# RWKV-style attention and a gated MLP on one core: three f-tiles begun with the tokens of steps 0 and 1, the second group's attention placed later, and y made as rows of x from step 3 on

## The chip, the core and the metric

One NeuronCore of a Trainium2 chip runs the whole program. Its engines work side by side, each on its own instruction queue, in order: TensorE (PE in the profile, its weight loads PEld), VectorE (DVE), ScalarE (ACT), GpSimd (POOL) and SyncE (SP), whose queue issues most of the DMAs. The metric is the device time of one execution in microseconds; smaller is better.

## The reference

Two parts follow each other. A linear attention runs over 768 tokens with one 48x48 state for each of 4 batches and 8 heads; its output, 3072 tokens by 384, goes through an MLP of 2048 hidden columns with a gate.

```python
for t in range(S):                       # S = 768, B = 4, H = 8, D = 48
    kt, vt, rt = (k[:, :, t], v[:, :, t], r[:, :, t])
    cur = np.einsum('bhd,bhe->bhde', u[None] * kt, vt)
    y[:, :, t] = np.einsum('bhd,bhde->bhe', rt, state + cur)
    state = w[None, :, :, None] * state + np.einsum('bhd,bhe->bhde', kt, vt)
...
x = np.ascontiguousarray(y.transpose(0, 2, 1, 3)).reshape(B * S, H * D)
h = x @ w_in                             # 384 -> 2048
sp = np.where(h > 20.0, h, np.log1p(np.exp(np.minimum(h, 20.0))))
g = h * np.tanh(sp)
return (g @ w_out).astype(np.float32)    # 2048 -> 384
```

## The kernel before

**The attention** is cut into 24 steps of 128 tokens (64 tokens of two batches). Step s multiplies r and k by tables of powers of w (`scale`, L483, on DVE), makes scores k·r for all heads on PE (`scores`, called from `attend`), keeps the part below the diagonal (L594, copies by a mask on DVE), and moves the pieces into two alternating sets of operands G, Wt and KI (`halves`: by ACT or DVE for steps 0 to 2, by DMAs of SP, L471, afterwards). `outputs(s)` then makes y (from G and Wt) and the new state st (from Wt and KI) on PE; the state goes back into Wt (L680). A step so needs the state of the step before it.

The term with u, which stands on the diagonal, is made in one of two ways. For s < UDIAG (6) the keys times u are scored a second time (`diag`, L504 or L502, and a second call of `scores`), and a second masked copy puts that diagonal in. From UDIAG on DVE works out the diagonal alone (L512, L516, L520, L525) from k and r loaded in the other layout.

**From y to x.** The MLP wants x with its 384 features on partitions. For s < TURN (6) `tokens` makes y with tokens on partitions; ACT copies it out (L693, L695), PE transposes it in three pieces (`transposes`, L751), ACT copies the result into x (L720), and in every group but the first DVE writes a second part (L723). From TURN on `rows` makes y with features on partitions at once; `direct` copies it into x with two ACT copies (L734) and two DVE subtractions (L737), and six small DMAs on SP's queue (L743) put the features of the fourth head pair where they belong.

**The MLP** has eight groups of three steps, 384 tokens each, and 16 f-tiles of 128 hidden columns in each. `up` makes one f-tile of h (hp in PSUM, two buffers), it is copied out (L892), four f-tiles form a batch of gate work on ACT (three activations with their table loads, L813, L816, L819) and DVE (L828), and `down` adds the f-tile to the output (acc, three PSUM tiles). In group 0 up and down are fp32 products with the weights whole (L802, L847: three k-tiles, six records of the profile for each f-tile); from group 1 on, weights and inputs are split in two parts and three products replace one (L778). The weights come as 16 pieces of 64-bit numbers and are converted to fp32 on ACT and DVE (L340 to L368) while group 0 runs, and are split afterwards (L383, L385).

**Who sets the order.** `Flow` is a planner that runs while the program is built. Each thread (load_step, scale, diag, keys, attend, outputs, evacuate, gate, ...) yields the events that it waits for and then what engine it wants and for how long; the planner gives the engine to the thread that can begin first by its cost table, and among equals to the lowest rank. The order that comes out is the order of every engine's queue, and the chip keeps to it whatever the real durations are. `place(s, piece)` says after which up tile (event `u<n>`) a step's scores (piece 0), outputs (piece 1) and, for the last step of a group, transposes (piece 2) may be put on PE: the 16 up tiles of the group before it are used from a share LO to a share HI, for group 1 LO0 and HI0. `rank(s)` follows from `place`, so a later place also means that the step's DVE and ACT work comes behind more of the other work. `ffn` is one thread that gives up tile n and then the down tiles that AFTER allows; in group 0 the first down tile comes after up tile 7. `up_tile` waits for x of the three steps of its group, and the first tile of the third batch (up tile 8) waits until the first batch is gated. While no up tile has been placed, `keep_warm` fills PE's idle time with products of zeros (L283).

At the start `state_decay` writes the diagonal of w**64 into KI[0] (L263, eight ACT instructions), and the thread `second_decay` writes the same into KI[1] by eight more, which `outputs(1)` waits for.

```python
    lo, hi = (LO0, HI0) if g == 1 else (LO1, HI1)
    at = (2 * (s - starts[g]) + piece) / (2 * GROUPS[g])
    return n0 + min(n - 1, int((lo + at * (hi - lo)) * n))
```

Of the kernel before, what the change touches and what calls it, by code (L numbers as in the profile page):

```python
# [22 lines left out]
NP = H // 2  # L23
# [4 lines left out]

TURN = 6


SOON = 3
LENT = 2

UDIAG = 6

# [11 lines left out]
WG = 2  # L48
# [20 lines left out]
LAG_US = 24.9  # L69
LO0, HI0, LO1, HI1 = 0.05, 0.9, 0.05, 0.8  # L70
AHEAD, HOLD_W = 2, 8
# [111 lines left out]
def pe(us):  # L183
    return {"pe": us}
# [3 lines left out]
def rwkv_mish_kernel(ctx, tc, rkT, rkN, vN, wT, w_in, w_out, consts, rkF, vF, wF, uF, outT):  # L188
# [70 lines left out]

    def state_decay(i, par, p):  # L260

        r = DROWS[par]
        nc.scalar.activation(  # L263
            KI[i][r, par, :, p, :], ident[r, r].unsqueeze(1).broadcast_to([D, 2, D]), AF.Copy, scale=w64[r, p : p + 1]
        )
# [11 lines left out]

    idle = ps.tile([128, 512], F32, name="idle", tag="hp", bufs=2)

# [8 lines left out]
    for par in range(2):  # L288
        for p in range(NP):
            state_decay(0, par, p)  # L290
    token_table()
# [4 lines left out]
    ok = const.tile([32, 1], I32, name="ok")  # L296

    def second_decay():
        for par in range(2):
            for p in range(NP):  # L300
                yield {"act": 0.3}
                state_decay(1, par, p)
        flow.set("decay")

# [93 lines left out]
    def load_step(s):  # L398
        i, q = divmod(s, NQ)
        before = s - RK_BUFS - (LENT < s <= LENT + RK_BUFS)  # L400
        if before >= 0 and s != LENT:
            yield f"moved{before}"
            yield f"placed{before}"
            yield f"keys{before}" if before < TURN else f"x{before}"
        yield {"sp": 1.28}
        if not spare:
            spares()
        rk = [128, 2, 2, NP, C]
        n = [128, 2, 2, NP, D]
# [81 lines left out]
    def diag(s):  # L491
        yield f"rkn{s}"
        if s < UDIAG:
            flow.set(f"rku{s}")
            yield f"scaled{s}"
            if s >= 2:
                yield f"scores{s - 2}"
            engine = yield {"act": 0.8, **dve(512)}
            k, to = rks[s][:112, 1], spare["ku"][s % 2][:112]
            if engine == "act":  # L500
                for p in range(NP):
                    nc.scalar.activation(to[:, :, p], k[:, :, p], AF.Copy, scale=uw[:112, p : p + 1])  # L502
# [56 lines left out]
    def attend(s):  # L559
# [6 lines left out]
        if GROUPS[0] <= s < UDIAG:  # L566
            yield f"state{s - 1}"
        if s > TURN:

# [5 lines left out]
        rk = loaded[s][0]  # L575
        if s <= TURN:
            yield from paced(s, 0)
# [52 lines left out]
    def outputs(s):  # L630
        q = s % 2
        last = s >= NS - NQ

        more = TURN <= s < NS - 1
        yield f"moved{s}"
        yield f"placed{s}"
        yield f"keys{s}"
        yield f"v{s}"
        if s == 1:
            yield "decay"  # L640
        if s:
# [84 lines left out]
    def direct(s, y):  # L726
        g, x, at = yield from new_x(s)

        last = loaded[s][1].rearrange("a m c p d -> a (m c p d)")[:, : 2 * ST].rearrange("a (m t) -> a m t", m=2)
        last = last.bitcast(F32R)  # L730
# [25 lines left out]
    def place(s, piece):  # L756

        if s > TURN and not piece:
            return place(s - 1, 1)
# [32 lines left out]
    def by_tile(o, t):  # L792
        return t[:, : o.n * o.T].rearrange("p (j t) -> p j t", j=o.n)

    def up(o, j):
        f, T = o.f + j, o.T
        hp = ps.tile([128, 512], F32, name="hp", tag="hp", bufs=2)
        w = (wholes if o.whole else parts)[0, f // WG]
# [55 lines left out]
    def put(engine, mt, T, cols):  # L854
# [4 lines left out]
        (nc.scalar.copy if engine == "act" else nc.vector.tensor_copy)(out=ob[:, :T], in_=accs[mt][:, :T])  # L859
        nc.scalar.dma_start(outT[mt * 128 : (mt + 1) * 128, cols], ob[:, :T])  # L860

# [3 lines left out]
    def up_tile(n):  # L865
# [9 lines left out]
        if n >= 2:  # L875
            yield f"h{n - 2}"
        yield pe(unit_us(n))
        flow.fill = None
# [96 lines left out]
    flow.start(load_weights(), -500, 0.0)  # L975
    flow.start(second_decay(), -1000.5, 0.0)
    for c in range(len(W_ORDER)):
# [4 lines left out]
        n += NF  # L982
        flow.start(split(c), (AFTER[n] - L_OUT if i else n - L_IN) + c / 1000, 0.0)
    flow.start(ffn(), 1000, 0.0)
    flow.run()
# [153 lines left out]
```

## Time and profile before

| | |
|---|---|
| runs, us | 529.8, 531.26, 535.85 (median 531.26) |
| the profiled execution, us | 530.0 |
| its span in the profile, us | 528.2 |
| mean granted TensorE clock | 0.994 |
| first up tile begins (L802), us from the span's start | 33.94 |
| first down tile begins (L847) | 56.53 |
| first up tile of group 1 (L778) | 101.26 |
| last product ends | 521.91 |

The span is what the profiler saw between the first and the last instruction; the time of that execution is 1.8 us longer. Times in views of the trace are counted from the span's start.

### The profile page before, as it was taken

The page shows a single profiled execution, that of the slowest core. Times are in us where ns is not written, and L with a number is a line of the kernel's source. Part 1 is how long each engine was busy: PE and PEld are TensorE (multiplying, and loading weights), DVE is VectorE, ACT ScalarE, POOL GpSimd, SP SyncE. Part 2 cuts the span into 40 slices and gives each one's busy share as a digit, 9 for nine tenths or more (in the row PEclk, how much of TensorE's full clock was granted, in tenths as well). Part 3 has the DMA queues.
Part 4 walks back from the last instruction along what each step waited for, and adds up shares of the span by engine and source line. Part 5 has one row for each costly group of instructions (what it writes and reads, how often), then busy time and mean ns, then how long its engine had stood idle before and what let it go on. Part 6 is the DMA issues. An engine that isn't in the chain of part 4 may idle for free.

```text
span 528.2 us, 11442 instructions
## 1 busy us (share of the span) xinstructions
PE 510.8 (97%) x4765; PEld 470.1 (89%) x4765; DVE 323.3 (61%) x489; ACT 402.8 (76%) x501; POOL 6.0 (1%) x19
## 2 busy tenths in 40 slices
PE   8887999999999999999999999999999999999994
PEld 6754666687999999999999999999999999999993
DVE  6998998765676575474664475474474473334341
ACT  6999957669798668667887768667687767777882
POOL 4000000000000000000000000000000000000000
PEclk9999899999999999999999999999999999999998
DMA  8998444113443244323443243323333250001001
GB/s 238 414 374 274 130 132 130 45 37 92 115 115 106 59 149 114 86 74 103 119 114 104 63 151 108 97 59 107 117 116 104 66 153 17 2 2 45 1 0 49
DMA packets 31051, 57.88 MB, mean 110 GB/s; under 512 B 6064, under 2 KB 19248, under 8 KB 30992
## 3 DMA queue, kind: packets, MB, share of 16 engines
q1 hardware_dynamic: 27392, 52.13, 33.9%
q10 hardware_dynamic: 3600, 4.95, 2.7%
q8 instruction: 39, 0.64, 0.5%
q14 instruction: 20, 0.16, 0.1%
HBM read 36.80 MB, written 4.72 MB: 79 GB/s over the span
## 4 chain that ended last, share of the span: by engine, by line
PE 80%; ACT 7%; DVE 4%; DMA 3%; SPq 2%; issue 2%; ACTq 0%; DVEq 0%
PE hp L778 30%; PE acc L778 27%; PE hp L802 6%; PE acc L847 5%; PE pa L554 5%; PE yt L620 3%; PE st L664 2%; SPq L743 1%; DMA rk<-in_rkT_dram 1%; ACT fa L816 1%; PE yt L607 1%; ACT wraw L340 1%; DMA rkn<-in_rkN_dram 1%; ACT L819 1%; DVE hb L828 1%
## 5 line engine op out<-in xcount | busy, mean ns | idle before, releaser
L778 PE MATMUL hp<-x,w 128*128 128x384 f32 x1008 | 197.0, 338 | 0.5 <-DMA x<-rkn 0.5
L778 PE MATMUL acc<-gh,w 128*128 128x384 f32 x672 | 187.8, 335 | 1.0 <-ACT gh L831 1.0
L778 PEld LDWEIGHTS hp<-x,w 128*128 128x128 f32 x1008 | 175.6, 188 | 3.8 <-DMA x<-rkn 0.8
L778 PEld LDWEIGHTS acc<-gh,w 128*128 128x128 f32 x672 | 122.8, 188 | 1.4 <-ACT gh L831 1.3
L778 PE MATMUL acc<-gl,w 128*128 128x384 f32 x336 | 112.3, 334 | 0.1
L892 ACT COPY hb<-hp 128x384 f32<-128x384 f32 x100 | 47.3, 474 | 59.6 <-PE hp L778 47.0
L828 DVE TENSOR_TENSOR hb<-hb,fa 128x768 f32<-128x768 f32 (+1 forms) x58 | 51.8, 927 | 39.9 <-ACT fa L819 39.9
L892 DVE COPY hb<-hp 128x384 f32<-128x384 f32 x28 | 15.6, 557 | 86.8 <-PE hp L778 84.1
L778 PEld LDWEIGHTS acc<-gl,w 128*128 128x128 f32 x336 | 63.1, 188 | 0.4 <-DVE gl L834 0.4
L831 ACT CAST gh<-hb 128x768 fp32r<-128x768 f32 (+1 forms) x58 | 47.2, 817 | 21.0 <-DVE hb L828 20.8
L834 DVE TENSOR_TENSOR gl<-hb,gh 128x768 fp32r<-128x768 f32 (+1 forms) x58 | 52.7, 928 | 7.6 <-ACT gh L831 5.8
L813 ACT ACTIVATE fa<-hb,bias_ln 128x1536 f32<-128x1536 f32 (+1 forms) x33 | 50.9, 1541 | 0.4
L816 ACT ACTIVATE fa<-fa 128x1536 f32<-128x1536 f32 (+1 forms) x33 | 47.8, 1449 | 2.0 <-ACT ob L859 1.7
L819 ACT ACTIVATE fa<-fa 128x1536 f32<-128x1536 f32 (+1 forms) x33 | 47.8, 1449 | 0.4
L819 ACT ACT_TABLE_LOAD x33 | 42.3, 1283 | 0.6
L813 ACT ACT_TABLE_LOAD x33 | 42.3, 1283 | 0.6
L483 DVE TENSOR_TENSOR rk<-rk,TRK 112x1024 f32<-112x1024 f32 x23 | 28.1, 1222 | 14.3 <-DMA rk<-in_rkT_dram 14.3
L847 PE MATMUL acc<-g,wraw 128*128 128x384 f32 x96 | 34.5, 496 | 0.0
L802 PE MATMUL hp<-x,wraw 128*128 128x384 f32 x96 | 33.2, 492 | 0.9 <-ACT x L720 0.9
L554 PE MATMUL pa<-rk 48*64 48x64 f32 x736 | 26.6, 222 | 4.7 <-DVE rk L483 3.5
L554 PEld LDWEIGHTS pa<-rk 48*64 48x64 f32 x736 | 23.4, 135 | 7.6 <-DVE rk L483 4.1
L802 PEld LDWEIGHTS hp<-x,wraw 128*128 128x128 f32 x96 | 18.4, 196 | 11.9 <-ACT x L720 1.1
(88 smaller groups left out, 452.5 us busy)
## 6 DMA issues: line engine op xcount, KB each, us to landing
rk<-in_rkT_dram SPq DMA_DIRECT2D x23, 448.0 KB, 4.2
rkn<-in_rkN_dram SPq DMA_DIRECT2D x18, 384.0 KB, 3.9
wraw<-in_w_in_dram SPq DMA_DIRECT2D x8, 768.0 KB, 12.1
wraw<-in_w_out_dram SPq DMA_DIRECT2D x8, 768.0 KB, 15.8
G<-rk SPq DMA_DIRECT2D x36, 128.0 KB, 2.3
out_dram<-ob ACTq DMA_DIRECT2D x24, 192.0 KB, 2.2
Wt<-in_vN_dram SPq DMA_DIRECT2D x46, 96.0 KB, 2.6
G<-rk SPq DMA_DIRECT2D x42, 96.0 KB, 2.4
```

Source lines behind the costliest of these rows:

```text
L483: nc.vector.tensor_tensor(out=rk[:112], in0=rk[:112], in1=TRK[:112].unsqueeze(2).broadcast_to([112, 2, 2, NP, C]), op=ALU.mult)
L554: nc.tensor.matmul(pa[TROWS[par], n : n + C], lhsT=keys[r, c, p, :], rhs=rk[r, 0, c, p, :], start=True, stop=True)
L778: nc.tensor.matmul(out, lhsT=a, rhs=m, start=first and n == 0, stop=last and n == 2)
L802: nc.tensor.matmul(hp[:, :T], lhsT=w[:, fs], rhs=o.x[:, 0, k, :T], start=k == 0, stop=k == KT - 1)
L813: nc.scalar.activation(o.g, o.hb, AF.Sigmoid, bias=bias_ln2, scale=1.0)
L816: nc.scalar.activation(o.g, o.g, AF.Arctan)
L819: nc.scalar.activation(o.g, o.g, AF.Sin, scale=2.0)
L828: nc.vector.tensor_tensor(out=to[:, j], in0=o.hb[:, j], in1=o.g[:, j], op=ALU.mult)
L831: nc.scalar.copy(out=o.gh[:, j], in_=o.hb[:, j])
L834: nc.vector.tensor_tensor(out=o.gl[:, j], in0=o.hb[:, j], in1=o.gh[:, j].bitcast(F32), op=ALU.subtract)
L847: nc.tensor.matmul(accs[mt][:, :T], lhsT=w[:, ws], rhs=o.gh[:, j], start=first, stop=last)
L892: (nc.scalar.copy if engine == "act" else nc.vector.tensor_copy)(out=o.hb[:, j], in_=h)
```

## The change

The order of the work and a few of its parts change; what is computed stays.

- `up_early`: f-tiles 0, 1 and 2 of group 0 are multiplied with the 256 tokens of steps 0 and 1 as soon as x of these is there; `up` then adds only the last 128 tokens. Each such tile is 2 x 3 products in place of 3. Tile 2 is put into the PSUM tile of acc0, and the products of zeros write to acc1 in place of hp.
- TURN goes from 6 to 3: steps 3, 4 and 5 use `rows` and `direct`. JOIN (6) keeps the other role of TURN, which step's scores are issued by the step before.
- UDIAG goes from 6 to 5: step 5 works its diagonal out on DVE.
- LO0 goes from 0.05 to 0.25. By `place`, scores and outputs of steps 3, 4, 5 may come after up tiles 4, 5 / 7, 9 / 10, 12, where before it was 0, 3 / 5, 7 / 9, 12.
- KI[1] is copied from KI[0] by four GpSimd copies (the loop stands twice) in place of the eight ACT instructions of `second_decay`.
- Of the last group's output, what DVE copied out is stored from SP's queue in place of ACT's.

```diff
-TURN = 6
+TURN = 3
+
+JOIN = 6
...
+EARLY = 3
...
-UDIAG = 6
+UDIAG = 5
...
-LO0, HI0, LO1, HI1 = 0.05, 0.9, 0.05, 0.8
+LO0, HI0, LO1, HI1 = 0.25, 0.9, 0.05, 0.8
...
-    idle = ps.tile([128, 512], F32, name="idle", tag="hp", bufs=2)
+    idle = ps.tile([128, 512], F32, name="idle", tag="acc1")
...
+    for par in range(2):
+        r = DROWS[par]
+        nc.gpsimd.tensor_copy(KI[1][r, par], KI[0][r, par])
+    for par in range(2):
+        r = DROWS[par]
+        nc.gpsimd.tensor_copy(KI[1][r, par], KI[0][r, par])
     token_table()
...
-    def second_decay():
-        for par in range(2):
-            for p in range(NP):
-                yield {"act": 0.3}
-                state_decay(1, par, p)
-        flow.set("decay")
...
-            yield f"keys{before}" if before < TURN else f"x{before}"
+            yield f"keys{before}" if before < UDIAG else f"x{before}"
...
+            if s - 2 >= TURN:
+                yield f"x{s - 2}"
...
-        if s > TURN:
+        if s > JOIN:
...
-        if s <= TURN:
+        if s <= JOIN:
...
-        more = TURN <= s < NS - 1
+        more = JOIN <= s < NS - 1
...
-        if s == 1:
-            yield "decay"
...
-        last = loaded[s][1].rearrange("a m c p d -> a (m c p d)")[:, : 2 * ST].rearrange("a (m t) -> a m t", m=2)
+        if s < UDIAG:
+            last = spare["ku"][s % 2].rearrange("a c p i -> a (c p i)")
+        else:
+            last = loaded[s][1].rearrange("a m c p d -> a (m c p d)")
+        last = last[:, : 2 * ST].rearrange("a (m t) -> a m t", m=2)
...
-        if s > TURN and not piece:
+        if s > JOIN and not piece:
...
+    def up_early(n):
+        g, f = UNITS[n][1:]
+        T = 128 * (GROUPS[g] - 1)
+        for s in range(GROUPS[g] - 1):
+            yield f"x{s}"
+        yield f"v0,{f // WG}"
+        yield pe(KT * 4 * T / 2400)
+        hps[n] = hp = ps.tile([128, 512], F32, name="hp", **(dict(tag="hp", bufs=2) if n < 2 else dict(tag="acc0")))
+        whole_up(hp, xs[g], f, slice(0, T))
+        flow.set(f"early{n}")
+
+    def whole_up(hp, x, f, at):
+        w = wholes[0, f // WG]
+        for k in range(KT):
+            fs = slice((k * WG + f % WG) * 128, (k * WG + f % WG + 1) * 128)
+            nc.tensor.matmul(hp[:, at], lhsT=w[:, fs], rhs=x[:, 0, k, at], start=k == 0, stop=k == KT - 1)
+
     def up(o, j):
         f, T = o.f + j, o.T
+        if o.whole and f in hps:
+            hp = hps.pop(f)
+            whole_up(hp, o.x, f, slice(T - 128, T))
+            return hp[:, :T]
...
-        nc.scalar.dma_start(outT[mt * 128 : (mt + 1) * 128, cols], ob[:, :T])
+
+        q = nc.sync if cols.stop == NT and engine == "dve" else nc.scalar
+        q.dma_start(outT[mt * 128 : (mt + 1) * 128, cols], ob[:, :T])
...
-        yield pe(unit_us(n))
+        if n < EARLY:
+            yield f"early{n}"
+        yield pe(unit_us(n) / (GROUPS[g] if n < EARLY else 1))
...
-    flow.start(second_decay(), -1000.5, 0.0)
...
+    for n in range(EARLY):
+        flow.start(up_early(n), n, 0.0)
```

More of the change, by code (lines that the diff above doesn't have):

```diff
@@ L258, in powers, with state_decay @@
             nc.vector.tensor_tensor(out=both(n, C - 2 * n, n), in0=both(0, C - n, n), in1=mul, op=ALU.mult)
-    def state_decay(i, par, p):
+    def state_decay(par, p):
         r = DROWS[par]
         nc.scalar.activation(
-            KI[i][r, par, :, p, :], ident[r, r].unsqueeze(1).broadcast_to([D, 2, D]), AF.Copy, scale=w64[r, p : p + 1]
+            KI[0][r, par, :, p, :], ident[r, r].unsqueeze(1).broadcast_to([D, 2, D]), AF.Copy, scale=w64[r, p : p + 1]
         )
@@ L289, in rwkv_mish_kernel @@
         for p in range(NP):
-            state_decay(0, par, p)
+            state_decay(par, p)
+    for par in range(2):
[4 more added lines that the diff above has]
+        nc.gpsimd.tensor_copy(KI[1][r, par], KI[0][r, par])
     token_table()
@@ L793, in by_tile @@
         return t[:, : o.n * o.T].rearrange("p (j t) -> p j t", j=o.n)
+    hps = {}
+    def up_early(n):
[13 more added lines that the diff above has]
+            nc.tensor.matmul(hp[:, at], lhsT=w[:, fs], rhs=x[:, 0, k, at], start=k == 0, stop=k == KT - 1)
     def up(o, j):
         f, T = o.f + j, o.T
+        if o.whole and f in hps:
+            hp = hps.pop(f)
+            whole_up(hp, o.x, f, slice(T - 128, T))
+            return hp[:, :T]
         hp = ps.tile([128, 512], F32, name="hp", tag="hp", bufs=2)
```

## The prediction

> **What bounds the kernel now.** I read the page first, its busy shares, then the windows of the first 110 us, then the timeline of the same stretch engine by engine, then the waits of PE, and last the timeline's end.
>
> ```profile
> PE 510.8 (97%) x4765; PEld 470.1 (89%) x4765; DVE 323.3 (61%) x489; ACT 402.8 (76%) x501; POOL 6.0 (1%) x19
> ...
> 16.00:24.00 8.00, 7.19 (x199) 6.31 (x197) 7.78 (x15) 7.63 (x14) 0.00 (x0) 1.00 1.02 415
> 24.00:32.00 8.00, 6.49 (x143) 5.41 (x140) 7.38 (x13) 7.85 (x17) 0.00 (x0) 1.00 1.02 346
> ...
> 50.00:52.00 2.00, 0.05 (x1) 0.00 (x0) 1.91 (x3) 1.99 (x2) 0.00 (x0) 1.00 0.41 101
> 52.00:54.00 2.00, 0.43 (x14) 0.43 (x16) 2.00 (x4) 2.00 (x4) 0.00 (x0) 1.00 0.02 7
> 54.00:56.00 2.00, 2.00 (x52) 2.00 (x48) 2.00 (x3) 1.98 (x6) 0.00 (x0) 0.60 0.35 95
> 56.00:58.00 2.00, 2.00 (x15) 1.35 (x12) 2.00 (x4) 1.99 (x2) 0.00 (x0) 0.55 0.44 107
> ```
>
> The page says PE, at 97%; but that is an average. In the windows the columns are start and end, length, then busy time of PE, PEld, DVE, ACT and POOL, the granted clock and the DMA share. Before 34 us the work runs through DVE and ACT, each 92 to 98% busy in 16 to 32 us, while PE's busy time is partly products of zeros. At 50 us PE stands still, and then gets only 0.60 and 0.55 of its clock for two windows of 2 us: 0.40 x 2 + 0.45 x 2 = 1.7 us lost beside the stop. After that PE is full to the end, so there time is PE work. The chain of events at the stop, from the timeline:
>
> ```profile
> 28.21 0.48 ACT L720 COPY x<-t 128x384 f32<-128x384 f32 x1
> 28.46 1.17 PE L607 MATMUL yt<-Wt,G 128*64 128x48 f32 x32
> 30.42 0.72 PE L283 MATMUL idle<-zeros 128*128 128x256 bf16 x5
> 31.99 0.55 PE L751 MATMUL t<-cst,G 128*128 128x128 f32 x3 [0.85 <-ACT G L695]
> 33.41 0.48 ACT L720 COPY x<-t 128x384 f32<-128x384 f32 x1
> 33.94 2.21 PE L802 MATMUL hp<-x,wraw 128*128 128x384 f32 x6 [0.86 <-ACT x L720]
> 36.23 13.82 PE L802 MATMUL hp<-x,wraw 128*128 128x384 f32 x42
> 42.35 0.48 ACT L892 COPY hb<-hp 128x384 f32<-128x384 f32 x1 [0.61 <-PE hp L802]
> 50.89 1.48 ACT L819 ACTIVATE fa<-fa 128x1536 f32<-128x1536 f32 x1
> 52.30 1.22 DVE L483 TENSOR_TENSOR rk<-rk,TRK 112x1024 f32<-112x1024 f32 x1
> 53.57 1.32 PE L554 MATMUL pa<-rk 48*64 48x64 f32 x32 [3.52 <-DVE rk L483]
> 53.91 1.82 DVE L828 TENSOR_TENSOR g<-hb,fa 128x768 f32<-128x768 f32 x2
> 56.53 2.82 PE L847 MATMUL acc<-g,wraw 128*128 128x384 f32 x6
> ```
>
> x of step 1 is there at 28.69, x of step 2 at 33.89. Eight up tiles run without a pause from 33.94 to 50.05. The fourth is copied out at 42.83, and its batch of gate work lasts until 52.37 on ACT, so PE is out of work at 50. It then waits 3.52 us for step 3's L483, behind which stands L828, the gate's last piece; the first down tile begins at 56.53. What of this stretch can be shortened is what the change is worth; what it saves later is PE work alone.
>
> **The change part by part.** The sum is made against the profiled execution, 530.0 us (span 528.2); the median of the runs is 1.3 above it.
>
> *Early tiles.* An up tile costs 13.82 / 7 = 1.97 us, two thirds of three tiles 3.95. Between x1 and x2 (28.69 to 33.94, 5.25 us) PE has yt and st of step 2, until 30.42, and transposes of 0.55; 3.0 us are free, the rest of the 3.95 pushes the transposes or the next step by some 1.0. The 128-token thirds cost more than a third: the nearest row is the 128-column transposes (81.20 to 81.62 below, 0.14 us each), 6 x 0.14 = 0.84 for 0.66, 0.5 us for three tiles. Gain 3.95 - 1.0 - 0.5 = 2.5. Ends: 0, if the tiles stand in PE's queue ahead of step 2's work (each 1.3 us, two of them, and the 0.5, eat most of it), and 3.9.
>
> *The second decay, and GpSimd.*
>
> ```profile
> L263 ACT ACTIVATE KI<-cst,pw 48x96 f32<-48x96 f32 x16 | 5.2, 364 | 2.7 <-DVE iw L246 2.6
> L226 POOL MEMSET Wt<- 48x384 f32 x4 | 1.5, 418 | 0.1
> ...
> 5.30 2.35 ACT L263 ACTIVATE KI<-cst,pw 48x96 f32<-48x96 f32 x8 [2.60 <-DVE iw L246]
> 14.54 0.72 DVE L594 COPY_PREDICATED gl<-cst,pa 128x512 f32<-128x512 uint32 x1
> ```
>
> Eight of sixteen go from ACT: 5.2 - 2.35 = 2.85 us, in the stretch in which ACT and DVE bound the start and share copies. Half of it, 1.4, would come off if both share it evenly; I take 1.2, with ends 0 and 2.85. Four GpSimd copies of 48x384 begin when KI[0] is done, at 7.65. No trace here has such a copy; by the clearing of the same shape, 0.42 each, they end at 9.4. Behind them on GpSimd's queue stand the two clearings of the masked tile, about 1 us, and for those waits step 0's masked copy, at 14.54. So they cost nothing up to 1.4 us each (7.65 + 4 x 1.4 + 1.0 = 14.3). I take 0, the end above is 2 us.
>
> The Trainium skill's page "GPSIMD Engine Reference", section 1 (Specifications), speaks against this move: GpSimd shares its SBUF interfaces with VectorE and contends with DVE instructions that read two SBUF inputs, and L483 is such an instruction. No run shown here has a GpSimd read beside DVE work. If DVE stood still for all four copies, that would be 4 x 0.42 = 1.7 us, an estimate, and the sum by it 524.8.
>
> *Second group's attention later.* With a higher rank, L483 and L539 of step 3 no longer stand ahead of L828: its first half could end at 52.37 + 0.1 + 0.92 = 53.4 in place of 54.8, and the first down tile follow at once, not at 56.53 behind 64 score products at half clock. Those then cost their 2.0 us on PE at full clock (81.62 to 83.63 below). Net 56.53 - 53.4 - 2.0 = 1.1. Ends: 3.1, if the scores still fit in the stop, and -1.0, if they fall where PE waits for them again.
>
> *PE work from step 3 on.*
>
> ```profile
> 63.15 1.14 PE L607 MATMUL yt<-Wt,G 128*64 128x48 f32 x32
> 64.12 0.89 PE L664 MATMUL st<-Wt,KI 128*48 128x48 f32 x32
> 81.20 0.49 PE L751 MATMUL t<-cst,G 128*128 128x128 f32 x3
> 81.62 1.15 PE L554 MATMUL pa<-rk 48*64 48x64 f32 x32
> 82.60 1.10 PE L554 MATMUL pa<-rk,gl 48*64 48x64 f32 x32
> 83.63 2.21 PE L802 MATMUL hp<-x,wraw 128*128 128x384 f32 x6
> 89.64 1.14 PE L607 MATMUL yt<-Wt,G 128*64 128x48 f32 x32
> 98.39 0.56 DVE L723 TENSOR_TENSOR x<-t,x 128x384 fp32r<-128x384 f32 x1 [0.26 <-ACT x L720]
> 101.26 2.04 PE L778 MATMUL hp<-x,w 128*128 128x384 f32 x9
> 113.45 1.15 PE L620 MATMUL yt<-G,Wt 128*64 128x64 f32 x32
> 114.39 0.92 PE L664 MATMUL st<-Wt,KI 112*48 112x48 f32 x32
> 119.18 3.94 SPq L743 DMA_DIRECT2D x<-rkn  x6
> 152.39 1.15 PE L620 MATMUL yt<-G,Wt 128*64 128x64 f32 x32
> 165.13 0.77 PE L778 MATMUL hp<-x,w 128*128 128x384 f32 x3 [0.54 <-DMA x<-rkn]
> ```
>
> Three sets of transposes go, 0.42 each: 1.2. Step 5's second scores go, 82.60 to 83.63: 1.0. `rows` costs what `tokens` does, 0.94 against 0.97: 0. On DVE step 5 gains four instructions (L512, L516, L520, L525) for one masked copy and one product, and each of the three steps has one subtraction more. DVE is off the path once PE is full; I take 0, and what would be late if it weren't is x of step 5. On SP each of the three steps adds six issues, 3.94 us, in front of the next step's loads; those are a step ahead, so 0. Load 7 now also waits for x5; no product needs it before group 2.
>
> *x of step 5.* The first tile of group 1 needs it. Before, from y's products to x took 98.95 - 89.64 = 9.3 us, and PE had 101.26 - 89.64 = 11.6 us of work meanwhile. By the new way it is 165.13 - 152.39 = 12.7 us, and there PE waited 0.54. So here some 1.1 us of lateness, less what step 5 gains since `scores` of step 5 no longer waits for state 4 and y 4. I take a cost of 0.5; ends 0 and 5.
>
> *The end.*
>
> ```profile
> 522.39 0.48 ACT L859 COPY ob<-acc 128x384 f32<-128x384 f32 x1 [1.01 <-DVE ob L859]
> ```
>
> The last copy waits while ACT issues the store of DVE's copy; with SP issuing that one, it can start just after PE's last product at 521.91: 0.4 gained, ends 0 and 0.5.
>
> Sum: 2.5 + 1.2 + 1.1 + 1.2 + 1.0 + 0.4 - 0.5 = 6.9, so 523.1. The runs' median stands above the profiled one, and I write 523.5.
>
> **The rivals.**
>
> *The front gives nothing.* The gate of the first batch is ACT work between conversions, ACT is full, and an earlier up tile 3 only finds it occupied. Then the first down tile stays at about 56.5, the stop grows by what the early tiles gained, and only 1.2 + 1.0 + 0.4 = 2.6 are left: 527.4. For it: ACT 7.85 of 8 us at 24 to 32 and 1.99 of 2 in the stop. Against it: the planner puts the gate between conversions as soon as its inputs are there, and 2.85 us of ACT work are gone.
>
> The Trainium skill's page "TensorE: Matmul & The Clock Gate", the section on HAM oscillation, says that a pause of PE over about 3.4 us brings the clock back to half. The trace agrees with one case, 3.52 us and then 0.60. By that rule my forecast, with a stop of 53.4 - 50.05 = 3.4 us, lies at its edge, and the sum with 1.7 us lost again would be 525.2.
>
> *Slower: x of step 5 comes late.* Steps 3 to 5 are a chain: scores of step 3 at 53.57, y of step 5 at 89.64, x5 at 98.95. If the later place puts step 3's scores behind the first two down tiles and an up tile, some 6 us later than the stop allows, and each step costs as before, x5 comes at 98.95 + 6 - 3.7 (the front's gain) + 12.7 - 9.3 = 104.7. What is saved before group 1 is then lost, PE begins it 3.4 later than before, cold at 1.7, and keeps only the end's 0.4: 530.0 + 3.4 + 1.7 - 0.4 = 534.7. It turns slower from x5 at about 100 on. Against it: scores and outputs of steps 4 and 5 no longer wait for transposes or x.
>
> *GpSimd is slow.* At 2.0 us a copy instead of 0.42 the masked tile is ready at 7.65 + 8 + 1 = 16.7, step 0 is 2.1 late, and the whole follows: 525.6.
>
> **How the numbers follow.** Forecast 0.55, the front gives nothing 0.25, x5 late 0.12, GpSimd slow 0.08. 1% is 5.3 us, about what a measurement of this kernel can tell from no change. The forecast's own range is 519 to 527: its terms' ends do not all fall on one side. Most of it, 0.45 of 0.55, lies over 1% below, and so does half of the GpSimd case with 0.04: 0.49 faster. x5 late gives 0.11 slower. The rest is 0.40. The range, 518 to 530.5, leaves out about 0.1 on either side.
>
> **What would show it.** Right: six L802 records of 256 columns three times before 34 us and of 128 columns after x2; the first down tile near 50, with no L483 before L828; no window under 0.9 of the clock; no L751 after step 2; the first L778 near 96 with no long wait. Wrong: a stop of over 3.5 us before the first L847, or an idle PE ahead of the first L778 on a DMA into x, or step 0's masked copy waiting on POOL.

## The result, and the profile after

| | before | after |
|---|---|---|
| median of 12 runs, us | 531.38 | 528.44 (526.5 to 531.38) |
| the profiled execution, us (its span) | 530.0 (528.2) | 529.33 (527.6) |
| first down tile begins | 56.53 | 49.62 |
| first up tile of group 1 begins | 101.26 | 100.83 |

The ratio of after to before is 0.9948, with an interval of 0.9926 to 0.997: 0.5% or 2.8 us, where 6.9 were forecast. It lies within 1%, and inside the range. In the profiled executions the first down tile comes 6.9 us earlier; of that, 0.43 is left at group 1's start, and the last product even ends 0.18 later (522.09 for 521.91). These two executions, 0.7 us apart, show little of the 2.9 between the medians: the one after is the fourth slowest of its twelve. So the question is where the lead of 6.9 went.

The line numbers have moved: up is L832 (its early and late pieces L819), down L877, the products of group 1 L785, `scale` L486, the gate's last piece L858, `rows` L625, SP's pieces L474, the stores of x L750, the loads L418 and L430.

First the page's line of busy time, then windows of 8 us of the kernel after (columns as in the prediction).

```profile
PE 508.2 (96%) x4716; PEld 468.6 (89%) x4716; DVE 321.3 (61%) x488; ACT 402.0 (76%) x502; POOL 10.0 (2%) x23
```

```profile
48.00:56.00 8.00, 6.38 (x20) 4.02 (x21) 7.59 (x11) 7.97 (x10) 0.00 (x0) 1.00 0.28 63
...
72.00:80.00 8.00, 7.28 (x56) 4.34 (x55) 7.17 (x14) 7.01 (x5) 0.00 (x0) 1.00 0.35 84
80.00:88.00 8.00, 6.51 (x97) 4.62 (x98) 5.47 (x10) 2.97 (x6) 0.00 (x0) 1.00 0.75 198
88.00:96.00 8.00, 5.60 (x57) 3.46 (x53) 8.00 (x14) 3.91 (x7) 0.00 (x0) 0.79 0.27 68
```

The stop at 50 us is shorter and its clock is whole: 1.00, where before had 0.60 and 0.55. But a new hole stands at 72 to 96. PE is busy 7.28 + 6.51 + 5.60 = 19.4 of 24 us there, so it stands still for 4.6, and at 0.79 of the clock the last window loses another 0.21 x 8 = 1.7. That is 6.3 us given back. The account closes to within about 1 us: 6.9 us of lead at the first down tile, less 2.0 since step 3's scores are not yet done there, is 4.9; the transposes and second scores that PE no longer makes give about 2.2; 4.9 + 2.2 - 6.3 = 0.8, and 0.7 more since the clock before was still at 0.55 behind its first down tile (0.45 x 1.47). Group 1 begins 0.43 earlier.

The timeline of PE shows both places, the front as forecast and then the hole. (The row of 18 records begins with the third early tile's six of 256 columns; its other twelve are of 128.)

```profile
29.80 2.64 PE L819 MATMUL hp<-x,wraw 128*128 128x256 f32 x11
32.60 2.87 PE L819 MATMUL hp<-x,wraw 128*128 128x256 f32 x18
35.56 0.97 PE L819 MATMUL hp<-x,wraw 128*128 128x128 f32 x6
...
49.62 2.18 PE L877 MATMUL acc<-g,wraw 128*128 128x384 f32 x6 [3.40 <-issue]
57.53 1.15 PE L559 MATMUL pa<-rk 48*64 48x64 f32 x32
...
75.58 1.15 PE L559 MATMUL pa<-rk 48*64 48x64 f32 x32
...
87.23 1.18 PE L625 MATMUL yt<-G,Wt 128*64 128x64 f32 x31 [1.49 <-DMA G<-rk]
91.58 3.62 PE L832 MATMUL hp<-x,wraw 128*128 128x384 f32 x6 [2.40 <-DVE wraw L371]
...
100.83 2.02 PE L785 MATMUL hp<-x,w 128*128 128x384 f32 x9
```

PE waits for step 5's masked scores (87.23), and then 2.40 us for a weight conversion on DVE. Both lead back to SP's queue; here is its timeline, then the step in the chain of waits, and the page's sizes of the transfers (KB each, median us from issue to landing).

```profile
72.81 3.90 SPq L750 DMA_DIRECT2D x<-gl  x6
76.82 1.17 SPq L474 DMA_DIRECT2D G<-gl  x2
78.09 1.19 SPq L474 DMA_DIRECT2D KI<-rkn  x2
79.38 0.53 SPq L418 DMA_DIRECT2D rk<-in_rkT_dram  x1
79.95 0.44 SPq L430 DMA_DIRECT2D rkn<-in_rkN_dram  x1
80.76 1.12 SPq L474 DMA_DIRECT2D G<-rk  x2
```

```profile
80.76 6.33 DMA G<-rk
```

```profile
rk<-in_rkT_dram SPq DMA_DIRECT2D x23, 448.0 KB, 4.2
rkn<-in_rkN_dram SPq DMA_DIRECT2D x19, 384.0 KB, 4.0
...
G<-rk SPq DMA_DIRECT2D x38, 128.0 KB, 2.3
```

```profile
73.14 0.74 DVE L599 COPY_PREDICATED gl<-cst,pa 128x512 f32<-128x512 uint32 x1
...
79.99 0.74 DVE L599 COPY_PREDICATED rk<-cst,pa 128x512 f32<-128x512 uint32 x1
...
84.47 1.23 DVE L486 TENSOR_TENSOR rk<-rk,TRK 112x1024 f32<-112x1024 f32 x1 [1.53 <-DMA rk<-in_rkT_dram]
...
86.90 0.56 DVE L517 TENSOR_TENSOR rkn<-rkn,cst 128x384 f32<-128x384 f32 x1 [1.01 <-DMA rkn<-in_rkN_dram]
```

The last fence is DVE's timeline. Step 4's mask is done at 73.88, yet its piece leaves SP only at 76.82: the six stores of step 3's x, 3.90 us, stand ahead of it. Step 5's scores (75.58) are masked by 80.73. Load 6 (832 KB) leaves right before them, and they land 6.33 us after their issue, where 2.3 is the median. DVE, in order too, stands 2.5 us for load 6's r and k, with the conversion that PE needs (L371) behind.

### The profile page after: what moved, and what is told of

The parts are those of the page before. It is cut to its first block, busy times and chain, and to the rows that moved or that the text cites. A ratio compares the mean times of both kernels' runs of the same rounds, so it can differ in the third digit from the quotient of the medians.

```text
span 527.6 us, 11377 instructions
## 1 busy us (share of the span) xinstructions
PE 508.2 (96%) x4716; PEld 468.6 (89%) x4716; DVE 321.3 (61%) x488; ACT 402.0 (76%) x502; POOL 10.0 (2%) x23
## 4 chain that ended last, share of the span: by engine, by line
PE 73%; ACT 14%; DVE 6%; DMA 4%; issue 1%; SPq 0%; DVEq 0%; ACTq 0%
PE hp L785 30%; PE acc L785 27%; PE pa L559 4%; PE yt L625 3%; PE acc L877 3%; PE st L667 2%; ACT fa L843 2%; ACT fa L849 2%; ACT L849 2%; ACT fa L846 2%; ACT L843 1%; DMA rkn<-in_rkN_dram 1%; PE hp L819 1%; DMA G<-rk 1%; ACT hb L926 1%
## 5 line engine op out<-in xcount | busy, mean ns | idle before, releaser
L785 PE MATMUL hp<-x,w 128*128 128x384 f32 x1008 | 197.0, 338 | 0.6 <-issue 0.5
L785 PE MATMUL acc<-gh,w 128*128 128x384 f32 x672 | 188.4, 335 | 1.1 <-ACT gh L861 1.0
L785 PEld LDWEIGHTS hp<-x,w 128*128 128x128 f32 x1008 | 175.6, 188 | 3.8 <-DMA x<-rkn 0.8
L785 PEld LDWEIGHTS acc<-gh,w 128*128 128x128 f32 x672 | 122.9, 188 | 2.1 <-ACT gh L861 1.3
L785 PE MATMUL acc<-gl,w 128*128 128x384 f32 x336 | 112.3, 334 | 0.1
L926 ACT COPY hb<-hp 128x384 f32<-128x384 f32 x105 | 49.4, 473 | 50.7 <-PE hp L785 43.1
L858 DVE TENSOR_TENSOR hb<-hb,fa 128x768 f32<-128x768 f32 (+1 forms) x58 | 51.8, 927 | 39.4 <-ACT fa L849 39.4
L785 PEld LDWEIGHTS acc<-gl,w 128*128 128x128 f32 x336 | 63.1, 188 | 0.4 <-DVE gl L864 0.4
L926 DVE COPY hb<-hp 128x384 f32<-128x384 f32 x23 | 12.8, 557 | 78.0 <-PE hp L785 77.8
L486 DVE TENSOR_TENSOR rk<-rk,TRK 112x1024 f32<-112x1024 f32 x23 | 28.4, 1237 | 15.2 <-DMA rk<-in_rkT_dram 15.2
L877 PE MATMUL acc<-g,wraw 128*128 128x384 f32 x96 | 34.3, 493 | 3.4 <-issue 3.4
L877 PEld LDWEIGHTS acc<-g,wraw 128*128 128x128 f32 x96 | 18.6, 198 | 14.1 <-issue 4.9
L832 PE MATMUL hp<-x,wraw 128*128 128x384 f32 x78 | 28.4, 511 | 2.4 <-DVE wraw L371 2.4
L625 PEld LDWEIGHTS yt<-G,Wt 128*64 128x64 f32 (+1 forms) x672 | 21.4, 130 | 8.8 <-issue 8.8
```

The costliest lines, as they stand in the source:

```text
L486: nc.vector.tensor_tensor(out=rk[:112], in0=rk[:112], in1=TRK[:112].unsqueeze(2).broadcast_to([112, 2, 2, NP, C]), op=ALU.mult)
L625: nc.tensor.matmul(y[par * C : par * C + m, n : n + C], lhsT=Wt[q][k].rearrange("k a c p e -> k (a c p e)")[:, at : at + m], rhs=G[q][k, p ...
L785: nc.tensor.matmul(out, lhsT=a, rhs=m, start=first and n == 0, stop=last and n == 2)
L858: nc.vector.tensor_tensor(out=to[:, j], in0=o.hb[:, j], in1=o.g[:, j], op=ALU.mult)
L877: nc.tensor.matmul(accs[mt][:, :T], lhsT=w[:, ws], rhs=o.gh[:, j], start=first, stop=last)
```

## The experiments

Each ratio is to the kernel before, measured on the same chip.

### Which of the parts holds group 1 back

**Step 3 to 5's stores of x on ACT's queue** (x_on_act).

```diff
-        yield {"sp": 3.6}
+        yield {"act": 2.4} if s < JOIN else {"sp": 3.6}
...
-                nc.sync.dma_start(
+                (nc.scalar if s < JOIN else nc.sync).dma_start(
```

> The change with the six small stores of x for steps 3, 4 and 5 issued from ACT's queue in place of SP's; the rest of SP's order stays. Theory A (SP's queue: the six stores of step 3, 3.9 us, stand ahead of step 4's masked scores and of load 6, and load 6 then lands ahead of step 5's masked scores): step 4's G store is issued near 74 in place of 76.8, y of step 5 near 83 in place of 87.2, no PE stop over 1 us at 79 to 92, first product of group 1 at 95 to 97 in place of 100.8, time 0.984 to 0.989 of before. Theory B (DVE's order: DVE waits 2.5 us for the loads of step 6 and a weight conversion comes late): the waits shrink only as far as load 6 comes earlier, 0.988 to 0.992. Theory C (the chain of steps 3 to 5 is too long from its start, whatever the queue): x of step 5 at 98 to 100 as now, 0.994 to 0.997.

Measured 0.998 [0.9958, 1.0002]. PE's timeline at group 1, and one window much later:

```profile
86.64 1.15 PE L625 MATMUL yt<-G,Wt 128*64 128x64 f32 x32
...
95.99 0.98 PE L785 MATMUL hp<-x,w 128*128 128x384 f32 x3
```

```profile
160.00:220.00 60.00, 56.55 (x547) 54.57 (x548) 35.35 (x52) 43.21 (x51) 0.00 (x0) 0.97 0.36 101
```

The hole is gone and group 1 begins 4.8 us earlier: without the six issues load 6 leaves 3.2 us before step 5's masked scores (77.76 and 80.97), and these land in at most 2.8 us. But the planner, given another cost, orders the later groups otherwise, and there PE stands still for 3.45 us, 1.4 of it on an output copy of DVE and the rest on x of step 8, and loses 0.03 x 60 = 1.8 of the clock. (The change itself has 59.34 of 60 there, at 1.00.) The time of the whole says nothing on the mechanism here; the trace up to 100 us does.

**Load 6 only after step 5's pieces have left SP** (load6_later).

```diff
+        if s == 6:
+            yield "placed5"
```

> The change with load 6 put behind step 5's masked scores in the plan (one more event that it waits for). Theory A: the store of step 5's masked scores lands 2.3 to 2.5 us after its issue in place of 6.3, y of step 5 at 83 to 84, first product of group 1 at 97 to 98.5, time 0.988 to 0.992 of before. Theory B: DVE's work of step 6 waits longer for its load or is planned later; if longer, PE's wait for the conversion grows over 2.4 us and the time is 0.995 to 1.000. Theory C: 0.994 to 0.997.

Measured 0.9914 [0.9882, 0.9947].

```profile
85.44 1.15 PE L627 MATMUL yt<-G,Wt 128*64 128x64 f32 x32
...
94.79 2.04 PE L787 MATMUL hp<-x,w 128*128 128x384 f32 x9
```

Then the landing times of the pieces put into G between 70 and 90 us, in the view of that tile:

```profile
DMA to landing us min/median/max: 2.2/2.3/2.4
```

No piece lands late any more (6.3 in the change), y of step 5 comes 1.8 us earlier, PE is full from 56 to 104 us, and group 1 begins 6.0 us before the change's. So load 6's place in SP's queue makes the hole, and the hole can go with the stores of x left where they are: step 4's piece still leaves behind 3.90 us of stores, at 75.97, and costs nothing. The planner also moves DVE's work of step 6 behind the later load, so the two waits, for the piece and on DVE, aren't told apart by this run. By spans this is 5.4 us faster than the change (522.2 to 527.6), by the ratios only 1.8, with intervals that overlap: the profiled execution, 524.06, is the fastest of its six. The windows of 48 to 56 us show the reason of a part of that, a cold clock:

```profile
48.00:56.00 8.00, 7.24 (x18) 4.25 (x19) 8.00 (x11) 7.97 (x12) 0.00 (x0) 0.79 0.32 79
```

**TURN back to 6** (turn_back: steps 3 to 5 by `tokens` and transposes, no such stores of x).

```diff
-TURN = 3
+TURN = 6
```

> The change with TURN at 6 again: steps 3 to 5 make y with tokens on partitions and transpose it, without the stores of x. Theory A: with no stores on SP the G store of step 4 is not held up; PE has 1.2 us more of transposes; first product of group 1 at 97 to 99, time 0.990 to 0.994 of before. Theory C: without the shorter way the steps wait for one another again, x of step 5 at 99 to 101, time 0.995 to 1.000.

Measured 0.9949 [0.9926, 0.9972], the change's own ratio. Group 1 begins at 100.55 there and at 100.83 in the change: the new way of making y from step 3 on gains nothing as the change has it. Without the stores on SP, theory A wanted group 1 at 97 to 99; the 99 to 101 of theory C came. Step 5's scores stand at 84.83, 9.2 us later than in the change, and PE waits 2.41 us for their piece though it lands in 2.4. The clock at the stop is 0.57 besides, 0.43 x 8 = 3.4 us that the change's own profile doesn't lose. So a chain that is late by itself ends at the same place as one that the queue holds up.

**No early tiles** (early_off).

```diff
-EARLY = 3
+EARLY = 0
```

> The change without the early tiles (EARLY 0). If the front's gain is all given back before group 1 (theories A, B and C agree in this for the kernel as it is), the first down tile comes at 53 to 56 in place of 49.6 and the first product of group 1 still at 100 to 102: time 0.994 to 0.999 of before. If the front's gain carries to the end, 1.000 to 1.006.

Measured 1.0023 [1.0003, 1.0044]. The first down tile comes at 52.17, 2.55 us later than in the change, just the 2.5 that the prediction gave the early tiles. Group 1, however, begins at 98.34, earlier than in the change: in this order there is no hole. Load 6 leaves 1.8 us before step 5's piece, which lands in 4.1 us, and y of step 5 stands behind more tiles (88.93). So the ratio falls where "the front's gain carries to the end" was put, but for another reason. The loss comes later (57.95 of 60 us busy in 160 to 220, clock 0.97), out of another order of the later groups.

### The front: the stop's clock, the order at the gate, the decays

warm_stop, its repeat stop_again and scores3 keep the later load 6; stop_only, lo0_back and decay_back stand beside the change alone.

**Twenty products of zeros in the stop** (warm_stop: `keep_warm` fills 2.35 of the 3.4 us, and the first down tile stands behind them).

```diff
+        if s == 6:
+            yield "placed5"
...
+        if n == 0:
+            keep_warm(20)
```

> The kernel load6_later with 20 products of zeros on PE behind up tile 7, in the stop ahead of the first down tile (some 2.2 us of the 3.4 us stop). Theory D (the stop lies at the clock gate's edge and costs a cold window in most executions): no window under 1.00 at 48 to 56 us, the first down tile takes 2.1 to 2.2 us in place of 3.1 to 4.2, time 0.986 to 0.990 of before. If the cold window is off the path because PE waits later anyway: 0.990 to 0.993, as load6_later.

Measured 0.9841 [0.9815, 0.9867]; run again:

> The kernel warm_stop once more, for its interval: 0.982 to 0.987 of before, if the first four executions were typical; 0.987 to 0.990 if they were lucky.

Measured 0.9848 [0.9818, 0.9877], 522.95 us beside 531.15. This beats both kernels. PE's timeline and windows of the second:

```profile
46.76 1.15 PE L287 MATMUL idle<-zeros 128*128 128x256 bf16 x9
49.12 2.18 PE L879 MATMUL acc<-g,wraw 128*128 128x384 f32 x6 [1.22 <-issue]
...
94.50 2.03 PE L787 MATMUL hp<-x,w 128*128 128x384 f32 x9
```

```profile
48.00:56.00 8.00, 6.88 (x22) 4.27 (x23) 7.94 (x11) 7.97 (x12) 0.00 (x0) 1.00 0.26 64
...
160.00:220.00 60.00, 60.00 (x583) 58.89 (x582) 35.88 (x52) 46.49 (x55) 0.00 (x0) 1.00 0.38 108
```

The products take nothing from the down tile, which waits for the gate anyway, and the clock stays whole.

**The same products without the later load 6** (stop_only).

```diff
+        if n == 0:
+            keep_warm(20)
```

> The change with the 20 products of zeros in the stop alone, load 6 where the change has it. Theory A and D together: the cold window at the first down tile goes, but step 5's y still waits for its G store behind load 6, so group 1 begins at 98 to 101 and little is kept: 0.991 to 0.995 of before. Rival, that load6_later's and warm_stop's gains are both the clock's: as warm_stop, 0.984 to 0.988.

Measured 0.993 [0.9905, 0.9956]. Beside the change the products alone give 0.002, with the load moved 0.007 (0.9914 to 0.9841 and 0.9848); the load alone gives 0.003, with the products 0.008 to 0.009. Each alone is within the noise of the change; the steps from one to both are clear of it. What PE gains ahead of y5 is lost again while it waits for y5, whose chain runs over SP and DVE: the hole is there in this run too (6.21 and 5.79 of 8 us in the windows from 80 to 96).

**Step 3's scores as soon as its r and k are loaded**, ahead of the stop (scores3, beside the later load 6).

```diff
-        if s < SOON:
+        if s <= SOON:
...
-        yield f"rkn{s}"
+        yield f"rk{s}" if s == SOON else f"rkn{s}"
...
+        yield f"rkn{s}"
...
-        rk = loaded[s][0]
+        rk = rks[s]
```

> The kernel load6_later with step 3's scaling and second keys planned as soon as its r and k are loaded, so that its scores stand after up tile 5 on PE, ahead of the stop. Theory E (after the queue is put right, what bounds group 1's start is when step 3 begins): step 3's scores at 44 to 46 in place of 58, y of step 5 4 to 8 us earlier, stop under 2.5 us, first product of group 1 at 91 to 94, time 0.983 to 0.988 of before. Rival: DVE has no room there, the scaling holds up the conversions or the gate, and the first down tile comes 1 to 2 us later: 0.990 to 0.995.

Measured 1.0 [0.9981, 1.0019].

```profile
41.80 1.15 PE L562 MATMUL pa<-rk 48*64 48x64 f32 x32
...
69.39 4.21 PE L835 MATMUL hp<-x,wraw 128*128 128x384 f32 x6 [5.64 <-DVE wraw L371]
```

The scores stand where they should, 15.7 us earlier than in the change, but DVE's work for the steps then comes ahead of its weight conversions, and an up tile waits 5.64 us for one. The rival named the cause, but neither the place nor the price: the first down tile isn't late (49.17), and 1.0 lies above its 0.990 to 0.995. DVE, "off the path", has no room for work brought forward.

**LO0 back to 0.05** (lo0_back).

```diff
-LO0, HI0, LO1, HI1 = 0.25, 0.9, 0.05, 0.8
+LO0, HI0, LO1, HI1 = 0.05, 0.9, 0.05, 0.8
```

> The change with LO0 at 0.05 again. The order of PE's, ACT's, SP's and GpSimd's queues comes out the same, and one DVE instruction stands one place apart, so what the later place was to bring is nothing: 0.993 to 0.997 of before, as the change, the first down tile at 49 to 50.5 with L858 ahead of step 3's L486. My prediction's step (the later place takes L483 from ahead of L828) would want the first down tile 1 to 3 us later.

Measured 0.9934 [0.9912, 0.9956]. Every engine's order is that of the change but for one instruction of DVE. DVE's timeline still has the gate first:

```profile
48.27 1.83 DVE L858 TENSOR_TENSOR g<-hb,fa 128x768 f32<-128x768 f32 x2 [0.42 <-ACT fa L849]
...
52.69 1.22 DVE L486 TENSOR_TENSOR rk<-rk,TRK 112x1024 f32<-112x1024 f32 x1
```

So the later place did not bring that about. early_off and decay_back have L858 first as well; no part taken back alone restores the order of before, and which of them made the new one stays open.

The one DVE instruction is step 5's mask, here ahead of both halves of a gate's L858 and in the change between them. Its piece lands as late (6.1 us), yet group 1 begins at 98.68, 2.1 us before the change's: PE stands still for 2.9 us in 80 to 96, and the clock is 1.00 there. So the hole's cold 1.7 us isn't in every execution, and a difference of 2 us at group 1 can be the execution's.

**The second decay back on ACT** (decay_back: eight ACT instructions, no copies on GpSimd).

```diff
-    for par in range(2):
-        r = DROWS[par]
-        nc.gpsimd.tensor_copy(KI[1][r, par], KI[0][r, par])
...
+                state_decay(par, p, 1)
...
+    flow.start(second_decay(), -1000.5, 0.0)
```

> The change with the eight ACT instructions for KI[1] again and no GpSimd copies. My prediction's step: x of step 2 about 1.2 us later than with the copies, time 0.996 to 0.999. Rival: DVE's work beside the GpSimd copies is as much longer as ACT's is shorter, x of step 2 within 0.5 us, time 0.993 to 0.997.

Measured 0.9976 [0.9955, 0.9998], 0.0028 or 1.5 us above the change, with intervals that overlap. That difference can't be put down to the decays: group 1 begins at 96.30 here, 4.5 us before the change's (step 5's piece lands in 5.5 us, but y of step 5 stands behind one more tile), and the loss lies in 160 to 220 us (57.95 of 60 busy, clock 0.97). ACT's timeline has x of step 2 (33.09 + 0.48 = 33.57 in the change) at 34.71:

```profile
34.23 0.48 ACT L726 COPY x<-t 128x384 f32<-128x384 f32 x1
```

Nine profiles, the change's and eight others, have the same order up to 36 us, and x of step 2 moves in them with the granted clock of 16 to 24 us: 32.40 to 33.04 at 1.00 (lo0_back, turn_back, udiag_back, load6_later), 33.15 to 33.57 at 0.79 (the change, x_on_act, stop_again), 34.34 and 34.47 at 0.57 (warm_stop, stop_only). In decay_back the clock there is 1.00. At a like clock the copies on GpSimd so bring x of step 2 forward by 1.7 to 2.3 us.

### More products of zeros, and the kernel before with them

At the start, too, some profiles show a cold clock at 16 to 24 us, so in warm_both products were put ahead of step 1's scores as well, on top of warm_stop.

```diff
+            if s == 1:
+                keep_warm(14)
```

> The kernel warm_stop with 14 more products of zeros ahead of step 1's scores (1.6 us of the 1.7 us pause at 13.4 us). Theory F (that pause lets the clock down at 16 to 22 us in a part of the executions and holds back x of step 2 by about 1 us): no window under 1.00 before 24 us, x of step 2 at 32.0 to 33.0, time 0.979 to 0.984 of before. If the pause plays no part: 0.983 to 0.987.

Measured 0.9904 [0.9882, 0.9927], slower than with the stop's products alone. The clock is 1.00 from 8 to 24 us, but PE pauses elsewhere, the clock falls to 0.94 and 0.84 in the two windows from 24 to 40, and x of step 2 comes at 36.68, not at 32 to 33. The waits of PE:

```profile
PE st L671 <- issue: 2.4, 1, 2.4
...
PE yt L616 <- issue: 1.2, 1, 1.2
```

The profile puts nothing down as what they wait for, and what causes them stays open. Without the later load 6 (warm_only):

> The change with both sets of products of zeros, and load 6 where the change has it. It tells the clock's part from the queue's. Theory A with D: the clock's part at the front is not kept, since step 5's y still waits for its G store and x of step 5 sets group 1's start: 0.989 to 0.995 of before, first product of group 1 at 98 to 101. If the two add up: 0.986 to 0.990.

Measured 0.998 [0.9961, 0.9999], above both ranges, with group 1 at 101.73. With both sets and the later load, but no early tiles (warm_no_early):

> The kernel warm_both without the early tiles. If the early tiles' gain at the front carries to the end once queue and clock are put right (my prediction's first term, 2.5 us): 2 to 3 us slower than warm_both, 0.984 to 0.989 of before. If it is still given back at group 1: within 1 us of warm_both.

Measured 1.0043 [1.002, 1.0065], 7.4 us above warm_both and outside both ranges. Group 1 begins 1.4 us earlier than there (97.75 and 99.15), so what is lost is lost later: 160 to 220 us has 55.23 of 60 busy at a clock of 0.94. And the kernel before with the stop's products alone (before_warm; its idle tile in acc1, since hp is in use at the stop):

> The kernel before, with 20 products of zeros behind up tile 7 (and these products written to acc1). If the cold windows behind the 3.5 us stop cost their 1.7 us to the end: 0.996 to 0.998 of before. If x of step 5 sets group 1's start there too, the front's gain is given back: 0.999 to 1.001.

Measured 0.9967 [0.9945, 0.999]: 1.8 us at the most likely, by the same edit that gives 3.7 where the rest is in order. The profile doesn't show where: group 1 begins at 101.58, against 101.26 before. Its timeline still has a cold first down tile, after a wait of 1.34 us for step 3's L483:

```profile
55.87 3.81 PE L847 MATMUL acc<-g,wraw 128*128 128x384 f32 x6
```

### The parts again, with the queue mended or not

**No early tiles, with the later load 6 and the stop's products** (stop_no_early).

> The kernel warm_stop without the early tiles. If the first term of the prediction, 2.5 us, reaches the end where nothing takes it back: 0.988 to 0.992 of before, first down tile at 51.5 to 53. If the early tiles also set the order of the later groups for the better, as early_off beside the change hints: 0.993 to 1.000.

Measured 1.0025 [1.0004, 1.0047], above both ranges, 0.018 or 9.4 us above the same kernel with them. Group 1 begins at 97.40, 2.9 us after stop_again's 94.50 and 1.5 after warm_stop's 95.95, which is the same kernel; the clock in 16 to 24 us is 0.58 here, 0.79 in stop_again and 0.57 in warm_stop. Most of the rest stands in one stretch:

```profile
160.00:220.00 60.00, 56.96 (x542) 54.34 (x541) 34.59 (x51) 43.43 (x51) 0.00 (x0) 0.94 0.38 104
```

That is 3.0 us idle and 0.06 x 60 = 3.6 of the clock, 6.6 in all. The early tiles themselves are worth the 1.5 at a like clock (up to 2.9); the 6.6 is another order of the later groups, which the kernel before doesn't suffer from either (59.46 of 60, clock 1.00), so it is no gain of the change.

**UDIAG back to 6**, in the change (udiag_back).

```diff
-UDIAG = 5
+UDIAG = 6
```

> The change with UDIAG at 6: step 5's diagonal from second scores again. In SP's queue load 6 then stands ahead of step 5's work altogether, well before its masked scores. Theory A: the G store of step 5 lands within 2.5 us, no PE stop at 85 to 92, and the 1.0 us of second scores comes back: 0.990 to 0.994 of before. My prediction's term alone (1.0 us of PE work): 0.996 to 0.998.

Measured 1.0061 [1.0041, 1.0081], 0.0113 or 6.0 us above the change; neither range held. SP's timeline and PE's:

```profile
86.19 3.88 SPq L750 DMA_DIRECT2D x<-gl  x6
90.16 1.18 SPq L474 DMA_DIRECT2D G<-gl  x2
```

```profile
84.46 1.15 PE L559 MATMUL pa<-rk 48*64 48x64 f32 x32
...
94.42 1.15 PE L625 MATMUL yt<-G,Wt 128*64 128x64 f32 x32
...
103.72 2.35 PE L785 MATMUL hp<-x,w 128*128 128x384 f32 x6 [7.44 <-DMA x<-gl]
```

This is first of all the plan. For s < UDIAG `attend` also waits for the state of the step before, so step 5's scores stand behind y and st of step 4, at 84.46 in place of 75.58. SP's queue adds to it: DVE has step 5's second mask done at 87.47, and its piece leaves at 90.16, behind the six stores of step 4's x. PE doesn't wait for that piece, since it has tiles until y of step 5; but this comes 7.2 us later than in the change, and PE then stands still 7.44 us before group 1, for x of step 5.

## Why the prediction was right or wrong

The time, 528.44, lies in the range; the forecast was 4.9 us too low, and the case that came is "within 1%". (The measurement tells more than that 1%: its interval is 0.2% to either side.) None of the signs of being wrong came: the stop is 3.40 us, no PE wait ahead of group 1 is on a DMA into x, and step 0's masked copy doesn't wait on POOL. Of the signs of being right, the clock (0.79 in 16 to 24 and in 88 to 96) and the start of group 1 (100.83, not 96) failed.

- *The front* held nearly to the figure, the rival "the front gives nothing" didn't: the first down tile begins at 49.62, "near 50", and the gate's L858 stands ahead of L486. The early tiles' 2.5 measured 2.55 at the first down tile (early_off), and 1.5 to 2.9 at group 1 (stop_no_early). The credit was split wrongly: the 1.1 us given to the later place isn't its own, since with LO0 back at 0.05 the gate still comes first (lo0_back).
- *Decays on GpSimd*: 1.2 was taken, between 0 and 2.85; at a like clock x of step 2 comes 1.7 to 2.3 us earlier (decay_back), and what of it reaches the end no run shows. The copies were slower than the 0.42 taken, up to 1.55 us, but the masked copy didn't wait for them, as forecast.
- *The step that failed*: "On SP each of the three steps adds six issues, 3.94 us, in front of the next step's loads; those are a step ahead, so 0." The loads have the time, but on the same queue and behind the same issues stand the next step's pieces of G, and these are on the path y4, st4, y5, x5. The stores held step 4's piece by 2.9 us, which by itself costs nothing (load6_later), and let load 6 out just ahead of step 5's; that one took 6.33 us, DVE stood 2.5 on the load, and PE lost 4.6 and, cold, 1.7. With the queue relieved in either of two ways (x_on_act, load6_later) group 1 begins 4.8 and 6.0 us earlier than in the change's profile. Pairs with a like clock in 16 to 24 us give 3.8 to 4.8 (99.77 in stop_only to 95.95 in warm_stop, 98.68 in lo0_back to 94.79 in load6_later, 100.83 in the change to 95.99 in x_on_act), and in time the step from stop_only to stop_again is 4.4 us.
- *x of step 5* was therefore mis-sized: 0.5 was taken between 0 and 5, and about 4 to 5 is what it came to. The mechanism of the rival "x of step 5 comes late" is there, with the first y5 at 87.23 and not at its price: it was put down to step 3's scores, which are indeed 4 us later than before (57.53), and the queue wasn't in it.
- *Transposes gone, 1.2, and second scores of step 5, 1.0*: PE does save them. But the one is worth nothing net (turn_back has the change's own ratio) and the other 6.0 us in the change (udiag_back), since step 5's scores no longer wait for step 4's state. The prediction names this relief and gives it no figure.
- *The stop of 3.4 us at the clock's edge* was named and not put in the sum. In the change's own profile it costs nothing (3.40, clock 1.00). In load6_later (3.42) and lo0_back (3.41) the window is at 0.79, and products in the stop are worth 3.7 us, though 1.7 is all that such a window shows. The profiled execution is the fastest of load6_later's six; over all executions the mean granted clock is 0.991 there and 0.995 with the products (warm_stop, stop_again), which makes some 2.1 us, an estimate (0.004 x 523). The rest stays open.
- *The end's* 0.4: no run isolates it, but the rows show it. The last copy begins 0.48 us after the last product ended before (522.39 and 521.91) and 0.03 in the change (522.12 and 522.09).

## What to carry to other kernels

Moving a copy to a DMA is not free where its queue also carries the next link of a chain: list what stands behind the new issues on that queue, not only what they store, and look at what the queue lets out next. Time gained ahead of a wait counts only if the thing waited for comes earlier too; so test two edits together that each give little alone (here 0.003 and 0.002, both within the noise, together 0.010). Where a planner writes the order, compare the stretch in which the mechanism lies and not only the time of the whole, since another cost moves groups far behind it.

## What the hardware showed

**A small transfer behind two large ones.** Of 128 KB pieces that land in 2.3 us, the one issued within 1.4 us of 832 KB of loads on the same queue took 6.33. How long it takes goes with how close it follows: here are the times at which the second part of load 6 and then step 5's piece leave SP, and the longest landing of a piece of G from 70 to 84 us (us).

| run | load 6 | the piece | landing |
|---|---|---|---|
| lo0_back | 79.74 | 80.42 | 6.1 |
| the change | 79.95 | 80.76 | 6.3 |
| stop_only | 80.68 | 81.52 | 6.2 |
| decay_back | 79.30 | 80.46 | 5.5 |
| early_off | 80.65 | 82.47 | 4.1 |
| x_on_act | 77.76 | 80.97 | 2.8 |
| load6_later | 87.72 | 80.66 | 2.4 |

The share of the DMA engines in that stretch was full, in the windows of 2 us of the change:

```profile
82.00:84.00 2.00, 2.00 (x8) 1.21 (x7) 0.94 (x2) 1.88 (x5) 0.00 (x0) 1.00 1.01 283
```

**The clock after a pause.** Pauses of 3.39 to 3.42 us ahead of the first down tile left it whole in one profile, the change's, and at 0.57 or 0.79 in five (x_on_act, load6_later, turn_back, lo0_back, udiag_back), and shorter ones, 3.06 (decay_back) and 2.54 (early_off), were followed by a window at 0.79 as well. In before_warm the clock is at 0.50 from 56 to 58 us behind a pause of only 1.34 us and step 3's scores. The Trainium skill's page "TensorE: Matmul & The Clock Gate", section "HAM oscillation", puts the edge at about 3.4 us of idle PE; the three shorter pauses don't agree with it. In before_warm the small score products behind the pause may count as idle, which no run here tells apart; in early_off and decay_back PE has full tiles on both sides.

**GpSimd copies beside VectorE.** GpSimd's timeline in the change, four copies of one shape:

```profile
6.53 0.50 POOL L297 COPY KI<-KI 48x384 f32<-48x384 f32 x1 [0.87 <-ACT KI L267]
7.71 1.55 POOL L297 COPY KI<-KI 48x384 f32<-48x384 f32 x1 [0.68 <-ACT KI L267]
9.32 2.03 POOL L300 COPY KI<-KI 48x384 f32<-48x384 f32 x2
```

Beside the small products of L262 one takes 0.50 us; beside L486, from 7.67 to 10.34 on DVE, it takes up to 1.55. DVE pays too: two L486 take 2.67 together, 1.22 and 1.23 before, and a copy of 48x512 takes 0.61 for 0.42. The shares differ:

```profile
L486 DVE TENSOR_TENSOR rk<-rk,TRK x2: 1224/1375/1526, 7.7 to 8.8; 112x1024 f32<-112x1024 f32 x2
```

The first L486 is not slowed (1.22), the second by a quarter (1.53), the copy by almost half. The Trainium skill's page "GPSIMD Engine Reference", section 1 (Specifications), has the interfaces to SBUF shared, with contention against DVE instructions of two SBUF inputs; the trace agrees, but in these three rows DVE loses 0.4 us in all, and not the 1.7 that the prediction gives for a DVE that stands still.
